# An adding transfer and one long scan in place of nine short ones, in a kernel of decayed attention and a mixture of experts

## The chip, the core and the metric

The kernel runs on one core of one Trainium2 chip. A core has five engines, each with its own queue of instructions: TensorE (PE, matrix products), VectorE (DVE), ScalarE (ACT, functions from loadable tables), GpSimd (POOL) and SyncE (SP, which only issues transfers). Sixteen DMA engines move data for all queues. Each engine works through its queue in order; between engines, semaphores order the work. The metric is the device time of one execution in microseconds (us), as the median of several runs.

## The reference

Thirty-two heads (4 batches of 8), 768 steps, 48 features. A complex decay per feature is kept below 0.999 in size; a state matrix per head decays and takes up k v^T at each step, and its real part is read with q:

```python
mag = np.sqrt(a_re * a_re + a_im * a_im)
scale = np.minimum(mag, 0.999) / (mag + 1e-06)
a_re_n, a_im_n = (a_re * scale, a_im * scale)
for t in range(S):
    ar, ai = (a_re_n[:, :, t, :, None], a_im_n[:, :, t, :, None])
    new_re = ar * S_re - ai * S_im
    new_im = ar * S_im + ai * S_re
    kv = np.einsum('bhd,bhe->bhde', k[:, :, t], v[:, :, t])
    S_re, S_im = (new_re + kv, new_im)
    y[:, :, t] = np.einsum('bhd,bhde->bhe', q[:, :, t], S_re)
```

The 3,072 rows of y (384 features) then go through eight experts with a capacity of 384 tokens each. Logits come from `x @ w_gate`; all (token, expert) pairs are walked in order of falling logit, and a pair is taken if the token is free and the expert has room. Each expert computes `relu(x @ w1) @ w2`.

## The kernel before

The attention works in chunks of 128 steps (a unit, 24 of them), three units to a group; two groups are a batch, eight groups (0 to 7) in all. For a group the four inputs a_re, a_im, k, q lie as [128 partitions, 3, 384 steps]: eight heads of 16 features on the partitions, three such blocks side by side.

Since the decay is a product over steps, the kernel works with logarithms: the sum of log sizes within a chunk and the sum of angles. The stages of a group have short names in `elementwise` (L341 on):

- F1, F2 (ACT): squares of ar into s1 and of ai into s2. F6: s2 += s1. F3, F4 (DVE): ar times ai into p, and the mark of a negative ar.
- F5, F7, F8 (ACT): logarithms and an exponential, from which F11 (DVE) makes the tangent of the angle in p.
- F9 (DVE): `zi` = -0.5 min(log(mag^2), 2 log 0.999), minus the log decay. F10 (ACT): s2 = exp(-0.5 log(mag^2)) x 1e-6, that is 1e-6 over the size, the small term that the 1e-6 of the reference's denominator brings. The log decay to be summed has these two terms, zi and s2.
- S (DVE, L386 to L392): for each unit of the group and each of the three blocks one scan of 128 columns, which adds zi and s2 to the running sum and begins at zero: nine scans for a whole group.
- G1, G2 (ACT): the exponentials of minus and plus that sum. G3, G5 (DVE): q and k times them. G4: the last column of each chunk, the decay of the whole chunk.
- A1 (ACT): arctangent; N0 (DVE): scans of the angle, 384 columns each; N1, N2 and T1 to T3: reduction of the angle, sine and cosine into CS.

Then, for each unit, RK and RQ (DVE, `f<-kq,CS`) turn k and q; K (SP, eight transfers `KQ<-f`, one a head) stacks them with 96 features on the partitions; SC, FL, ST, CA, MX, FN (PE) make the scores, transposes, state and output, with MK (`am<-sc,mask`) and WM (`W<-U,KQ`) on DVE and KC, XC, XE on ACT between them; LR takes the logits.

In six groups (1 to 6, `BY_DMA`) F6 is already no DVE instruction but a transfer from SBUF to SBUF that adds, issued on POOL (`s<-s` in the profile). Groups 0 and 7 are cut in two pieces (`CUTS`) and do F6 on DVE.

What sets the order: all stages are entered as operations with an engine, a cost, their predecessors and a priority (the chunk's number plus an offset from the table `OFF`, one entry for each kind of stage, L641). `in_order` (L173 on) plays them through: whenever an engine is free, the ready operation with the lowest priority goes next. The code is emitted in that order, and a `Queue` holds every engine to it. An adding transfer counts there as an operation of POOL of 7.5 us for a whole group. ACT's functions lie in two tables, one with logarithm and exponential and one with arctangent and sine; `PLAN` says which stages of which group share a loading. Where PE would be idle by the plan, matrix products on a constant (`hot`) are put in. The experts behind have a planner of their own, which the change leaves alone.

Of the kernel before, what the change touches and what calls it, by code (L numbers as in the profile page):

```python
# [8 lines left out]
F32 = mybir.dt.float32  # L9
# [4 lines left out]
AF = mybir.ActivationFunctionType  # L14
OP = mybir.AluOpType
# [5 lines left out]
B, H, S, D = 4, 8, 768, 48  # L21
# [3 lines left out]
GC = 3  # L25
# [210 lines left out]
def attention(nc, real, tc, z, q, k, a_re, a_im, v_tok, xd, later):  # L236
    ctx = ExitStack()
    con = ctx.enter_context(tc.tile_pool(name="acon", bufs=1))
# [4 lines left out]
    ps = ctx.enter_context(tc.tile_pool(name="ps", bufs=1, space=PSUM))  # L243
    W, VT = [], []
    v, g = nc.vector, nc.gpsimd
    for i in range(2):
        w = con.tile([96, 400], F32, name=f"W{i}")
        g.memset(w, 0.0)
        W.append(w)
    for i in range(2):  # L250
        x = con.tile([128, GC, 432], F32, name=f"V{i}")
# [9 lines left out]
    act = nc.scalar.activation  # L261
# [4 lines left out]
    def op(key, eng, cost, prio, fn, deps=()):  # L266
        kind = key[0][0] if type(key[0]) is tuple else key[0]
        o = Op(eng, cost, fn, [made.get(d) for d in deps], prio)
        o.kind = kind + ("<" if prio < EARLY else ">" if prio >= LATE else "")
        ops.append(o)  # L270
        made[key] = o
        return o
# [4 lines left out]
    def scan_(n):  # L277
        return n * 2.15 / 960 + 0.06
# [4 lines left out]
    def sca(n, bias=False):  # L283
        return n / 1200 + (0.23 if bias else 0.14)
# [4 lines left out]
    def dma(nbytes):  # L289
        return nbytes / 2.6e5  # L290
# [6 lines left out]
    def get(name, gi, shape=None, p=ew, **kw):  # L297
        if (name, gi) not in tiles:
            tiles[name, gi] = p.tile(shape or [128, 3, T], F32, name=name, **kw)
        return tiles[name, gi]  # L300

    BUFS = dict(ar=1, ai=1, kq=KQ_BUFS, s1=S1_BUFS, s2=2, zi=2, p=2, neg=2, gc=3, CS=1)

# [3 lines left out]
    def free(name, stages, gi):  # L307
        return [x for s in stages for x in last_of(s, gi - BUFS[name])]
# [4 lines left out]
    def load_a(gi, j, name, src):  # L313
        b, c0, n = GROUPS[gi]
        lo, hi = cuts[gi][j]
        w = slice(lo * 128, hi * 128)
        t = slice(c0 * 128 + lo * 128, c0 * 128 + hi * 128)
        return lambda: nc.sync.dma_start(
            get(name, gi, p=ld, bufs=1)[:, :, w], src[b, :, :, t].rearrange("j p t -> p j t"))
# [21 lines left out]
    def elementwise(gi, j, at):  # L341
        b, c0, _ = GROUPS[gi]
        lo, hi = cuts[gi][j]
        n = hi - lo
        N3 = 384 * n
# [3 lines left out]
        def G_(name, **kw):  # L349
            return get(name, gi, **kw)[..., cols]  # L350
# [4 lines left out]
        def add(stage, eng, cost, fn, deps):  # L355
            op((stage, gi, j), eng, cost, at, fn, deps)

        def k_(*ss):
            return [(s_, gi, j) for s_ in ss]

        add("li", "dma", dma(128 * N3 * 4), load_a(gi, j, "ai", a_im), free("ai", ["F2", "F3"], gi))
        add("la", "dma", dma(128 * N3 * 4), load_a(gi, j, "ar", a_re), free("ar", ["F1", "F3", "F4"], gi))
        add("F1", "act", sca(N3, True), lambda: act(G_("s1", bufs=S1_BUFS), G_("ar"), AF.Square, bias=z.cb[:, 0:1]),
            k_("la") + free("s1", ["F11", "F6"], gi))
# [7 lines left out]
            G_("neg", bufs=2), G_("ar"), 0.0, math.pi, op0=OP.is_lt, op1=OP.mult), k_("la") + free("neg", ["T1", "T2"], gi))  # L372
        if (gi, j) in BY_DMA:
            add("F6", "pool", 2.5 + 5.0 * n / GC, lambda: g.dma_start(out=G_("s2"), in_=G_("s1"), accum_op=OP.add), k_("F1", "F2"))
# [8 lines left out]
        add("F10", "act", sca(N3, True), lambda: act(G_("s2"), G_("s2"), AF.Exp, scale=-0.5, bias=z.cb[:, 3:4]), k_("F9"))  # L383
        add("F11", "dve", dve(N3), lambda: v.tensor_tensor(G_("p"), G_("p"), G_("s1"), op=OP.mult), k_("F8", "F3"))

        for c in range(n):  # L386
            def scan(c=c):
                t = slice(c * 128, c * 128 + 128)
                zi, s2 = G_("zi"), G_("s2")
                for i in range(3):  # L390
                    v.tensor_tensor_scan(zi[:, i, t], zi[:, i, t], s2[:, i, t], 0.0, op0=OP.add, op1=OP.add)
            add(("S", c), "dve", 3 * scan_(128), scan, k_("F10"))  # L392
        add("G1", "act", sca(N3), lambda: act(G_("s2"), G_("zi"), AF.Exp, scale=-1.0), [(("S", c), gi, j) for c in range(n)])
        add("G2", "act", sca(N3), lambda: act(G_("zi"), G_("zi"), AF.Exp), k_("G1"))
        add("G3", "dve", dve(N3), lambda: v.tensor_tensor(G_("kq")[:, 1], G_("kq")[:, 1], G_("s2"), op=OP.mult),
            k_("G1") + [("lk", gi)])
# [178 lines left out]
    for gi in range(G):  # L575
        for j in range(len(cuts[gi])):
            elementwise_at = gi * GC + cuts[gi][j][0]
            if j == 0:
                load(("lk", gi), 4.5, elementwise_at + 0.5, load_kq(gi), turned(gi - KQ_BUFS))
                if gi < 2:  # L580
                    load(("lv", gi), 2.2, elementwise_at + 0.6, load_v(gi))
            elementwise(gi, j, elementwise_at)
        for c in range(GC):
            turns(gi * GC + c)
            unit(gi * GC + c)
        if gi + 2 < G:
            load(("lv", gi + 2), 2.2, elementwise_at + 4, load_v(gi + 2),
                 [("MX", gi * GC + c) for c in range(GC)] + [("ST", gi * GC + c) for c in range(GC)])
# [8 lines left out]
    for o in ops:  # L597
        o.prio += OFF.get(o.kind, 0.0)
    hot = ps.tile([128, 512], F32, name="hot")
# [33 lines left out]
PLAN = [(0, 0, 1, 3), (0, 2, 1, 3), (2, 4, 3, 5), (4, 6, 5, 7), (6, 8, 7, 9), (8, 10, 9, 11), (10, 12, 11, 13), (12, 14, 13, 15), (14, 16, 15, 17), (16, 18, 17, 19)]  # L633
KQ_BUFS = 2
S1_BUFS = 2
BY_DMA = [(gi, 0) for gi in range(1, 7)]
SLACK = 0.0
DMA_WAIT = 1.5
DMA_DONE = 1.1
START = dict(pe=0.0, act=0.6, dve=1.5, pool=3.4, dma=0.0)  # L640
OFF = {"A1": 7.7532, "F1": -8.0, "F10": -0.2852, "F11": 6.1629, "F2": 1.0958, "F3": 3.1048, "F4": 3.0098, "F5": -8.0, "F6": 8.0, "F7": -6.5322, "F8": 3.2365, "F9": 5.0508, "FL": 2.946, "FL<": -3.9259, "FN": 4.3835, "G1": -0.6071, "G2": 4.4992, "G3": 8.0, "G4": -8.0, "G5": -5.9505, "K": 1.9006, "KC": -0.4768, "LR": -3.8173, "MK": -2.5243, "MX": -4.6482, "N0": 0.976, "N1": -8.0, "N2": -5.5169, "P0": -6.2872, "R0": -7.514, "R1": -4.516, "R2": 3.2639, "R3": 4.827, "R4": -4.8476, "R5": -0.5791, "S": 6.954, "SC": 3.4101, "SC<": -8.0, "ST": 0.3675, "ST<": -0.421, "T1": 7.9956, "T2": 6.9667, "T3": -8.0, "TL": 5.7027, "UA": -3.4084, "UA<": -5.1223, "WM": 0.1274, "XC": 7.799, "XC<": -7.3842, "XE": 4.4086, "XS": 0.7846, "la": -5.6357, "later": -8.0, "li": -5.3368, "lk": -1.3428, "lv": 6.2134, "RK": -2.7051, "RQ": -3.6666, "table": -0.5748, "CA": 3.7656, "BE": -7.9653}  # L641
CHAIN = ("scalar", "vector", "tensor", "gpsimd", "sync")
F_BUFS, KC_BUFS = 4, 5
SQ = ()
# [407 lines left out]
class Plan:  # L1052
# [13 lines left out]
    def add(self, eng, cost, outs, ins, fn):  # L1066
        deps = []
        for v, write in [(x, False) for x in ins] + [(x, True) for x in outs]:
            r = v.root
            for o, part, w in r.uses:  # L1070
                if (w or write) and (part is None or v.part is None or part == v.part):
                    deps.append(o)
            for old in r.older:
                deps += [u[0] for u in old.uses]
            if r.peer:
                deps.append(r.peer.uses[0][0])
        g = self.group
        if g is not None and g[0] is not None:
            o = g[0]
            assert o.eng == eng  # L1080
            o.deps += [d for d in deps if d is not o]
            o.cost += cost
            o.fns.append(fn)
        else:
            o = Op(eng, cost, None, deps, 0.0)
            o.fns = [fn]
            o.fn = lambda: [f() for f in o.fns]
            o.kind = self.kind
            self.ops.append(o)
            if g is not None:  # L1090
                g[0] = o
        for v, write in [(x, False) for x in ins] + [(x, True) for x in outs]:
            v.root.uses.append((o, v.part, write))
        return o
# [275 lines left out]
@with_exitstack  # L1370
def tile_decay_attention_then_capacity_moe(ctx, tc, q, k, a_re, a_im, v, w_gate, w1, w2, out):
    nc = tc.nc
    z = K()
    con = ctx.enter_context(tc.tile_pool(name="con", bufs=1))
    dp = ctx.enter_context(tc.tile_pool(name="dram", bufs=1, space=DRAM))
    xd = dp.tile([N, DM], F32)
    constants(nc, con, z, w_gate)
    router = Router(nc, z, con)
    queue = Queue(tc, nc, CHAIN)
    attention(queue, nc, tc, z, q, k, a_re, a_im, v, xd, router.constants())  # L1380
    experts(queue, tc, z, router, w1, w2, xd, out)
# [35 lines left out]
```

## Time and profile before

| | |
|---|---|
| median of 3 runs | 536.97 us (533.43 to 538.29) |
| the profiled execution | 535.22 us, span 533.4 us |
| busy, share of the span | PE 86%, DVE 79%, ACT 51%, POOL 16% |
| chain that ended last | PE 52%, DVE 16%, DMA 9%, issue 8%, ACT 5% |
| adding transfers `s<-s` | 6, of 576 KB each |
| first matrix product | 44.1 us |
| last logits of the attention | 244.2 us |

How to read what follows: the windows give, for stretches of the span, the busy time of each engine and the count of its instructions; the chain is followed back from the last instruction to what released it; a wait is put down to the one that came last. Instructions are named out<-in, with buffer numbers left out, so that `s` is s1 or s2. Nearly all carry L131, the line of the helper through which the queues pass; they are told apart by their names. Times of one instruction overlap the next by some 60 to 100 ns, so start-to-start is what a row of them costs.

### The profile page before, as it was taken

The numbers are of one execution on the slowest core, as the hardware profiler recorded it, in microseconds if no ns is written. First come the engines' busy times: TensorE is split into PE (matmuls) and PEld (weight loads), VectorE is DVE, ScalarE is ACT, GpSimd is POOL, SyncE is SP. The second block draws the span as 40 slices with busy tenths as digits, with TensorE's granted clock in tenths as the row PEclk, the third lists the DMA queues.
The fourth block names the chain that finished last, engine by engine and source line by source line (L and its number), as shares of the span: only waits on it lengthen the run. The fifth ranks groups of instructions, "written<-read, shape, count | busy, mean of one in ns | idle before, by whom it ended". The sixth has DMA issues, their size and how long they took to land.

```text
span 533.4 us, 9780 instructions
## 1 busy us (share of the span) xinstructions
PE 456.6 (86%) x3665; PEld 402.6 (75%) x3665; DVE 424.0 (79%) x1249; ACT 274.2 (51%) x426; POOL 84.5 (16%) x96
## 2 busy tenths in 40 slices
PE   0008989998989999995599898999999999999993
PEld 0007978686869889994498567898888888999993
DVE  8988689999989999835847779899898998944340
ACT  6995678796949695521012512342261723633430
POOL 3000000000000000000021322232341414620202
PEclk9999999999989999997589999999999999999998
DMA  7866858887978676621353403552260714830101
GB/s 226 264 182 156 222 164 270 224 228 245 257 216 267 197 237 169 192 75 45 110 174 123 173 31 122 190 215 82 78 250 29 265 34 190 320 138 4 45 1 44
DMA packets 48911, 86.06 MB, mean 161 GB/s; under 512 B 5344, under 2 KB 43744, under 8 KB 46816
## 3 DMA queue, kind: packets, MB, share of 16 engines
q1 hardware_dynamic: 39104, 42.56, 27.4%
q0 software_dynamic: 6304, 38.16, 21.2%
q10 hardware_dynamic: 3456, 4.72, 2.6%
q8 instruction: 29, 0.48, 0.4%
q14 instruction: 18, 0.15, 0.1%
HBM read 53.49 MB, written 9.44 MB: 118 GB/s over the span
## 4 chain that ended last, share of the span: by engine, by line
PE 52%; DVE 16%; DMA 9%; issue 8%; ACT 5%; SPq 4%; POOL 3%; POOLq 0%; DVEq 0%; ACTq 0%
PE acc L131 29%; PE y L131 5%; PE U L131 5%; PE sc L131 5%; SPq L131 4%; DMA s<-s 3%; DMA KQ<-f 3%; PE cnt L131 3%; ACT s L131 2%; DVE f L131 2%; PE xp L131 2%; PE kp L131 2%; DMA ai<-in_a_im 2%; DVE hl L131 1%; PE thr L131 1%
## 5 line engine op out<-in xcount | busy, mean ns | idle before, releaser
L131 PE MATMUL sc<-KQ 96*128 96x128 f32 x384 | 52.8, 293 | 41.7 <-DMA KQ<-f 41.6
L131 PEld LDWEIGHTS sc<-KQ 96*128 96x128 f32 x384 | 50.0, 207 | 45.1 <-DMA KQ<-f 42.6
L131 ACT ACTIVATE hh<-acc 128x384 fp32r<-128x384 f32 x56 | 27.4, 491 | 63.3 <-PE acc L131 61.9
L131 PE MATMUL acc<-w2l,hh 128*128 128x384 f32 x168 | 54.1, 346 | 0.0
L131 PE MATMUL acc<-w2h,hh 128*128 128x384 f32 x168 | 53.6, 345 | 0.0
L131 PE MATMUL acc<-w2h,hl 128*128 128x384 f32 x168 | 53.4, 343 | 0.0
L131 PE MATMUL acc<-xl,w1h 128*128 128x384 f32 x168 | 51.4, 344 | 0.0
L131 PE MATMUL acc<-xh,w1h 128*128 128x384 f32 x168 | 51.3, 345 | 0.0
L131 PE MATMUL acc<-xh,w1l 128*128 128x384 f32 x168 | 51.1, 343 | 0.0
L131 POOL DMA_INDIRECT out<-ot,idx x24 | 31.5, 1310 | 112.2 <-ACT ot L131 102.6
L131 DVE SCALAR_TENSOR_TENSOR hl<-acc,hh 128x384 fp32r<-128x384 f32 x56 | 30.4, 551 | 17.8 <-ACT hh L131 17.2
L131 DVE TENSOR_TENSOR f<-kq,CS 128x768 f32<-128x768 f32 x48 | 43.5, 951 | 0.2 <-ACT CS L131 0.2
L131 ACT ACTIVATE ot<-acc 128x384 f32<-128x384 f32 x24 | 11.7, 489 | 58.4 <-PE acc L131 50.1
L131 PE MATMUL y<-am,V 128*64 128x128 f32 x384 | 38.3, 289 | 1.1 <-ACT xT L131 0.6
L131 DVE TENSOR_TENSOR am<-sc,mask 128x512 f32<-128x512 f32 x48 | 32.2, 684 | 8.9 <-PE sc L131 8.8
L131 DVE TENSOR_TENSOR ind<-m,thr 128x768 bf16<-128x768 f32 (+1 forms) x40 | 33.7, 848 | 6.0 <-PE thr L131 5.8
L131 POOL DMA_INDIRECT w1t<-in_w,eidx x8 | 9.3, 1164 | 162.0 <-DVE of L131 118.7
L131 PE MATMUL U<-V,kt 128*96 128x48 f32 x320 | 32.4, 258 | 1.6 <-DVE tl L131 1.3
L131 PEld LDWEIGHTS U<-V,kt 128*96 128x96 f32 x320 | 31.6, 176 | 2.6 <-ACT kt L131 1.8
L131 PEld LDWEIGHTS acc<-xh,w1h 128*128 128x128 f32 x168 | 30.8, 188 | 2.6 <-issue 1.1
L131 PE MATMUL y<-KQ,W 96*64 96x128 f32 x320 | 31.8, 276 | 0.2 <-DVE W L131 0.2
L131 PEld LDWEIGHTS acc<-w2h,hh 128*128 128x128 f32 x168 | 31.1, 188 | 0.7 <-issue 0.4
(197 smaller groups left out, 1108.1 us busy)
## 6 DMA issues: line engine op xcount, KB each, us to landing
KQ<-f SPq DMA_DIRECT2D x192, 96.4 KB, 2.5
kq<-in_k SPq DMA_DIRECT2D x8, 576.0 KB, 5.1
kq<-in_q SPq DMA_DIRECT2D x8, 576.0 KB, 7.0
V<-in_v SPq DMA_DIRECT2D x8, 576.0 KB, 8.9
xd<-x ACTq DMA_DIRECT2D x24, 192.0 KB, 2.8
ar<-in_a_re SPq DMA_DIRECT2D x6, 576.0 KB, 4.6
ai<-in_a_im SPq DMA_DIRECT2D x6, 576.0 KB, 5.4
s<-s POOLq DMA_DIRECT2D x6, 576.0 KB
```

What stands on the lines that cost most here:

```text
L131: r = f(*a, **k)
```

## The change

In groups 1 to 6 (`SUM_BY_DMA`) the two terms of the log decay are summed ahead of the scan, by a second adding transfer on POOL: SD, zi += s2, behind F10. One scan over all 1,152 columns then takes the place of the nine. It multiplies the running sum by a constant, `again`, and adds zi; `again` is one everywhere and zero in the first column of each chunk, so that the sum begins anew there. G1 waits for this scan. The constant is filled on POOL at the start of the attention. The table of offsets is new throughout, with an entry for SD, so the order within the attention changes on all engines.

```diff
+    again = con.tile([128, 9 * 128], F32, name="again")
+    g.memset(again, 1.0)
+    g.memset(again.rearrange("p (a t) -> p a t", t=128)[:, :, 0], 0.0)
...
-        for c in range(n):
+        summed = (gi, j) in SUM_BY_DMA
+        if summed:
+            add("SD", "pool", 2.5 + 5.0 * n / GC, lambda: g.dma_start(out=G_("zi"), in_=G_("s2"), accum_op=OP.add), k_("F10"))
+
+            def scan_all():
+                x = G_("zi").rearrange("p a t -> p (a t)")
+                v.tensor_tensor_scan(x, again, x, 0.0, op0=OP.mult, op1=OP.add)
+            add(("S", 0), "dve", scan_(N3) + 0.12, scan_all, k_("SD"))
+        for c in range(0 if summed else n):
...
-        add("G1", "act", sca(N3), lambda: act(G_("s2"), G_("zi"), AF.Exp, scale=-1.0), [(("S", c), gi, j) for c in range(n)])
+        add("G1", "act", sca(N3), lambda: act(G_("s2"), G_("zi"), AF.Exp, scale=-1.0), [(("S", c), gi, j) for c in range(1 if summed else n)])
...
+SUM_BY_DMA = [(gi, 0) for gi in range(1, 7)]
...
-OFF = {"A1": 7.7532, "F1": -8.0, "F10": -0.2852, "F11": 6.1629, "F2": 1.0958, "F3": 3.1048, "F4": 3.0098,
...
+OFF = {"A1": 8.0, "F1": -1.706, "F10": -7.9433, "F11": 6.3823, "F2": -0.1719, "F3": 3.6663, "F4": 2.2339,
...
```

More of the change, by code (lines that the diff above doesn't have):

```diff
@@ L640 @@
 START = dict(pe=0.0, act=0.6, dve=1.5, pool=3.4, dma=0.0)
-OFF = {"A1": 7.7532, "F1": -8.0, "F10": -0.2852, "F11": 6.1629, "F2": 1.0958, "F3": 3.1048, "F4": 3.0098, "F5": -8.0, "F6": 8.0, "F7": -6.5322, "F8": 3.2365, "F9": 5.0508, "FL": 2.946, "FL<": -3.9259, "FN": 4.3835, "G1": -0.6071, "G2": 4.4992, "G3": 8.0, "G4": -8.0, "G5": -5.9505, "K": 1.9006, "KC": -0.4768, "LR": -3.8173, "MK": -2.5243, "MX": -4.6482, "N0": 0.976, "N1": -8.0, "N2": -5.5169, "P0": -6.2872, "R0": -7.514, "R1": -4.516, "R2": 3.2639, "R3": 4.827, "R4": -4.8476, "R5": -0.5791, "S": 6.954, "SC": 3.4101, "SC<": -8.0, "ST": 0.3675, "ST<": -0.421, "T1": 7.9956, "T2": 6.9667, "T3": -8.0, "TL": 5.7027, "UA": -3.4084, "UA<": -5.1223, "WM": 0.1274, "XC": 7.799, "XC<": -7.3842, "XE": 4.4086, "XS": 0.7846, "la": -5.6357, "later": -8.0, "li": -5.3368, "lk": -1.3428, "lv": 6.2134, "RK": -2.7051, "RQ": -3.6666, "table": -0.5748, "CA": 3.7656, "BE": -7.9653}
+OFF = {"A1": 8.0, "F1": -1.706, "F10": -7.9433, "F11": 6.3823, "F2": -0.1719, "F3": 3.6663, "F4": 2.2339, "F5": -7.7649, "F6": 5.849, "F7": 6.5769, "F8": -3.2078, "F9": 2.6695, "FL": 1.2547, "FL<": 8.0, "FN": 4.2725, "G1": -3.6349, "G2": -1.218, "G3": 7.3854, "G4": -3.8733, "G5": -4.3477, "K": 2.785, "KC": 1.3113, "LR": 0.9742, "MK": -0.6582, "MX": -7.3883, "N0": 1.9427, "N1": -6.0423, "N2": -8.0, "P0": 2.6412, "R0": -0.5866, "R1": -0.9225, "R2": -6.3991, "R3": 0.0469, "R4": -4.5019, "R5": 8.0, "S": 6.3482, "SC": 2.5769, "SC<": 6.1603, "ST": -3.0459, "ST<": -4.9702, "T1": 6.4264, "T2": -0.4648, "T3": -4.7434, "TL": 5.7714, "UA": -7.8876, "UA<": -0.6213, "WM": 0.079, "XC": 8.0, "XC<": 0.7027, "XE": 2.1979, "XS": 4.141, "la": -5.959, "later": 2.3562, "li": -5.1343, "lk": 1.3753, "lv": 4.4034, "RK": -2.0242, "RQ": -3.022, "table": -7.0509, "CA": 1.9062, "BE": -5.3127, "SD": 8.0}
 CHAIN = ("scalar", "vector", "tensor", "gpsimd", "sync")
```

## The prediction

> **What bounds the kernel now.** I read the windows by stage first, then the chain of waits, then who VectorE (DVE) waits for, then single instructions. The change sits in the attention part, which ends near 245 us of the 533.4 us span; the expert part behind it keeps its instructions, so only the first 245 us can move. Windows of 20 us (engine, busy us, instruction count; then granted clock, share of the 16 DMA engines, GB/s):
>
> ```profile
> core 0: us, PE busy (x) PEld busy (x) DVE busy (x) ACT busy (x) POOL busy (x), PEclk, DMA share, GB/s
> 40.00:60.00 20.00, 18.27 (x100) 16.74 (x102) 16.17 (x28) 14.08 (x16) 0.00 (x0) 1.00 0.71 198
> 60.00:80.00 20.00, 18.18 (x175) 15.70 (x173) 15.72 (x28) 12.14 (x17) 0.84 (x1) 1.00 0.65 163
> 80.00:100.00 20.00, 19.27 (x199) 15.77 (x199) 19.69 (x34) 18.00 (x20) 0.85 (x1) 1.00 0.92 275
> ...
> 140.00:160.00 20.00, 17.31 (x155) 14.42 (x154) 18.12 (x33) 13.08 (x16) 0.85 (x1) 0.91 0.83 231
> ...
> 220.00:240.00 20.00, 20.00 (x232) 18.30 (x228) 9.14 (x17) 5.62 (x12) 0.00 (x0) 1.00 0.41 110
> ```
>
> Three stages. From 40 to 80 us no engine is full: DVE idles 3.8 and 4.3 us. From 80 to about 200 DVE is nearly full. From 220 DVE is done and TensorE (PE) is full. The chain of waits shows the same (start, duration, what):
>
> ```profile
> 18.34 8.09 DMA s<-s
> ...
> 44.12 2.50 PE sc L131 x10
> ...
> 141.12 9.25 DMA s<-s
> ...
> 215.39 1.78 PE sc L131 x16
> ...
> 222.82 1.81 PE sc L131 x16
> 230.26 1.78 PE sc L131 x16
> ```
>
> Up to 44.1 the chain is latency, one adding transfer of 8.09 us in it. At the end the units of 128 tokens follow each other every 7.43 us (215.39, 222.82, 230.26), set by PE alone: the 24 units would fill 24 x 7.43 = 178 us, and attention takes some 200 us from 44.1. So about 20 us are DVE work and waits, and only these can shrink.
>
> **The change part by part.**
>
> *Nine scans become one.* DVE groups between 44 and 222 us, and a small scan from the whole span:
>
> ```profile
> L131 DVE TENSOR_TENSOR_SCAN zi<-zi,s 128x128 f32<-128x128 f32 x54 | 18.1, 400 | 0.0
> L131 DVE TENSOR_TENSOR_SCAN neg<-p,neg 128x384 f32<-128x384 f32 x9 | 7.9, 935 | 0.0
> ...
> L131 DVE TENSOR_TENSOR_SCAN rank<-ones,of,tie 128x24 f32<-128x24 f32 x7 | 1.8, 260 | 0.0
> ```
>
> The 54 scans cost 18.1 us, 0.335 each and 3.02 per group. One of 384 columns costs 7.9/9 = 0.878, so a column costs (0.878 - 0.335)/256 = 2.12 ns, and 1,152 columns 0.878 + 768 x 0.00212 = 2.51 us. Saved: 0.51 a group, 3.1 us in six. If the long scan only did as well as three of 384 (2.63), it would be 2.3. The new scan multiplies and adds; the `rank` scan is of that kind, and its 260 ns lie above the 400 - 104 x 2.12 = 180 that 24 columns of the other kind would take, so a start may cost 0.08 more, once a group. All columns are walked either way, so only starts are saved. Four of the six stand in the full stretch (2.0 of the 3.1), the first two among DVE's waits; I take **-3.1**, with the 2.0 as a bound.
>
> *The mask of ones.* It is filled on GpSimd (POOL) ahead of all its other constants:
>
> ```order
>  L59 ISA
>  L59 IOTA jp 128x128
>  L81 DMA pick<-in_w_gate 48x4x8 x2
> -L131 MEMSET W_110 96x400
> -L131 MEMSET W_112 96x400
> -L131 MEMSET V_114 128x3x48
> -L131 MEMSET V_116 128x3x48
> +L131 MEMSET again 128x1152
> +L131 MEMSET again 128x9
> +L131 MEMSET W_113 96x400
> +L131 MEMSET W_115 96x400
> +L131 MEMSET V_117 128x3x48
> ```
>
> So everything behind moves back by two fills, the ramp `jf` among it, for which DVE waits already:
>
> ```profile
> 3.15 0.85 POOL L131 MEMSET W<- 96x400 f32 x2
> 3.89 0.43 POOL L131 MEMSET V<- 128x144 f32 x2
> ...
> 5.22 0.15 POOL L131 IOTA jf<- 2x32 f32 x1
> ...
> 5.41 0.19 DVE L131 TENSOR_SCALAR start<-jf 1x32 bf16<-1x32 f32 x1 [0.20 <-POOL jf L131]
> ```
>
> ```profile
> 28.66 0.51 ACT L131 ACTIVATE p<-neg 128x384 f32<-128x384 int32 x1
> ```
>
> Two fills of 400 columns take 3.89 - 3.15 = 0.74, so 1,152 columns about 0.37 x 2.88 = 1.07, 1.1 with the second. Queued behind DVE's `start` is all of DVE's work on the first pieces, which leads through ScalarE (ACT) to the adding transfer of 18.34. Bounds for the first KQ: 0 (ACT absorbs it) to +1.1. One activation of 0.51 that stood behind that transfer's landing now stands ahead of it, so **+0.7**.
>
> *The transfer, and the scan's wait for it.* SD needs F10, and the scan needs SD. What an adding transfer costs by itself shows where the DMA engines carry nothing else (30 to 36 us, 40 slices, tenths; then the queue's share):
>
> ```profile
> 30.52 0.85 POOL L131 DMA_DIRECT2D s<-s  x1 [11.12 <-ACT s L131]
> ```
>
> ```profile
> DMA  0000000000001919699093990919969010000000
> ...
> q0 software_dynamic: 144, 0.59, 51.0%
> ```
>
> It takes 51% of 6 us, 3.06 us of all 16 engines, and is over in slice 33, at 35.0: landing 4.5 us after POOL began. Among other traffic the two of the chain took 8.09 and 9.25. DVE runs in order, so the question is how much work stands between F9 (`zi<-s`, after which ACT does F10) and the scan. The tightest place is group 5. Its DVE rows before, from F9 to the first scan (s_970 is its s2, now s_1040):
>
> ```order
> L131 TENSOR_SCALAR zi<-s_970 128x1152
> L131 COPY f<-gc 128x6
> L131 TENSOR_TENSOR p<-p,s_1034 128x1152
> L131 TENSOR_TENSOR W_110<-U,KQ 96x384
> L131 SCALAR_TENSOR_TENSOR zi<-zi,s_970 128x128 x3
> ```
>
> The same stretch of DVE now, from F9 to the scan:
>
> ```order
> L131 TENSOR_SCALAR zi<-s_1040 128x1152
> L131 COPY tl<-neg 128x3
> L131 TENSOR_TENSOR kq<-kq,s_758 128x1152
> L131 TENSOR_SCALAR neg<-neg 128x1152
> L131 COPY f<-gc 128x6
> L131 TENSOR_SCALAR neg<-neg 128x1152
> L131 TENSOR_TENSOR p<-p,s_984 128x1152
> L131 TENSOR_TENSOR W_113<-U,KQ 96x384
> L131 TENSOR_TENSOR am<-sc,mask 128x512 x2
> L131 TENSOR_TENSOR W_115<-U,KQ 96x384
> L131 SCALAR_TENSOR_TENSOR p<-ar,ai 128x1152
> L131 SCALAR_TENSOR_TENSOR zi<-again,zi 128x1152
> ```
>
> Three rows stood between the two, now ten. What these take, start to start, with F10 on ACT:
>
> ```profile
> 81.91 0.55 DVE L131 TENSOR_TENSOR W<-U,KQ 96x384 f32<-96x384 f32 x1
> 82.38 1.35 DVE L131 TENSOR_TENSOR kq<-kq,s 128x1152 f32<-128x1152 f32 x1
> 83.64 0.75 DVE L131 TENSOR_SCALAR zi<-s 128x1152 f32<-128x1152 f32 x1
> 84.31 1.35 DVE L131 TENSOR_TENSOR p<-p,s 128x1152 f32<-128x1152 f32 x1
> 85.58 1.28 DVE L131 TENSOR_TENSOR am<-sc,mask 128x512 f32<-128x512 f32 x2
> 86.78 1.05 DVE L131 TENSOR_TENSOR_SCAN zi<-zi,s 128x128 f32<-128x128 f32 x3
> ```
>
> ```profile
> 84.43 1.26 ACT L131 ACTIVATE s<-s,cb 128x1152 f32<-128x1152 f32 x1
> ```
>
> W 0.47, kq 1.26, a tensor_scalar 0.67, p 1.27, two am 1.20: between F9 and the scan of group 5 stand kq, two neg, two p, two W, two am and two copies (about 0.07 each), 1.26 + 1.34 + 2.54 + 0.94 + 1.20 + 0.14 = 7.4 us. F10 and landing need 1.3 + 4.5 = 5.8 at best, 1.3 + 8.1 = 9.4 or 1.3 + 9.25 = 10.6 among traffic. So DVE waits 0, 2.0 or 3.2 us, with the rotations f of the next units and their KQ transfers queued behind. For group 4 the same count gives 9.6 us of cover (wait 0 to 1.0), for group 2 10.2 (0 to 0.4); groups 1, 3 and 6 have far more. (For group 4: four am, one scan, W, p, two kq, four copies, one lg; group 2 has one neg more.) Together 0 to +4.6. The stretch is as loaded as that of the chain's two; I take the lower of them, **+2.0**. The Trainium skill, page "DMA: Bandwidth & Descriptors", section on the anatomy of a GpSimd DMA, gives 2.0 us plus bytes/436e9 for one: an estimate of 3.4 us for 589,824 bytes, by which no scan waits and the sum would be 2.0 lower. The 8.09 and 9.25 of this trace speak against it where the engines are loaded. On POOL each SD stands ahead of a later group's F6, but its F10 comes before that group's F2 on ACT, so F6 waits for nothing new.
>
> *The new order.* All priorities are new. DVE rows where group 1's rotations begin, before:
>
> ```order
> L131 TENSOR_TENSOR f<-kq,CS 128x6x128
> L131 TENSOR_TENSOR am<-sc,mask 128x512 x2
> L131 TENSOR_REDUCE lg<-xp 128x8
> L131 TENSOR_TENSOR f<-kq,CS 128x6x128 x2
> L131 TENSOR_TENSOR W_110<-U,KQ 96x384
> ```
>
> The same place now:
>
> ```order
> L131 TENSOR_TENSOR f<-kq,CS 128x6x128 x3
> L131 TENSOR_TENSOR am<-sc,mask 128x512 x2
> L131 TENSOR_REDUCE lg<-xp 128x8
> L131 TENSOR_TENSOR f<-kq,CS 128x6x128 x2
> L131 TENSOR_TENSOR W_115<-U,KQ 96x384
> ```
>
> A unit's KQ needs two f. All three f at the head now run together. Before, the second came after a wait for PE (instructions by start, duration):
>
> ```profile
> 62.06 0.95 DVE L131 TENSOR_TENSOR f<-kq,CS 128x768 f32<-128x768 f32 x1
> ...
> 67.10 1.82 DVE L131 TENSOR_TENSOR f<-kq,CS 128x768 f32<-128x768 f32 x2
> ...
> 68.07 8.27 SPq L131 DMA_DIRECT2D KQ<-f  x12
> ```
>
> Who DVE waited for between 44 and 80 us (total, times, longest):
>
> ```profile
> DVE am L131 <- PE sc L131: 4.7, 4, 2.2
> DVE W L131 <- PE U L131: 1.6, 1, 1.6
> DVE lg L131 <- ACT x L131: 1.5, 2, 1.4
> ```
>
> Now it ends at 62.06 + 2 x 0.87 = 63.8 instead of 68.0, so PE gets unit 3 up to 4.2 us earlier, out of the 7.8 us that DVE waits in 44 to 80 (the last three rows). Gain 0 to 4.2: ACT's tables and the loads must keep up too, so half, **-2.1**. Unit 0 loses a little, since the scan of group 1 now stands between its two am; that is inside the half. On SP one load now goes ahead of unit 2's KQ, one issue.
>
> *More traffic.* Six transfers of 3.06 us add 18.4 us of all 16 engines.
>
> ```profile
> 80.00:180.00 100.00, 94.12 (x923) 78.98 (x923) 94.69 (x166) 82.15 (x100) 2.54 (x3) 0.98 0.84 241
> ```
>
> Four fall here: share 0.84 + 0.12 = 0.96. Cost 0 if the pipeline's five KQ buffers cover it; upper bound in the rivals. I take **+0.5**.
>
> **Sum:** -3.1 + 0.7 + 2.0 - 2.1 + 0.5 = -2.0. The profiled execution took 535.22 us (span 533.4), 1.75 below the median of 536.97. Against its own time the sum gives 533.2; against the median, which the forecast is for, **535.0**.
>
> **The rivals.**
>
> *The adds land early (faster).* With 4.5 us no scan waits, and the lead of 4.2 us is kept whole: -3.1 + 0.7 - 4.2 = -6.6, **530.4**. For it: the transfer alone is that quick, and cover is 7.4 us or more. Against it: the share of 0.84 to 0.92 where it must land. The page's 3.4 us stands for this rival.
>
> *The DMA engines become the bound (slower).* Between 141 and 151 us the share was full, and the KQ transfers showed it (first row; the second is the whole span):
>
> ```profile
> KQ<-f SPq DMA_DIRECT2D x6, 96.4 KB, 6.4
> ...
> KQ<-f SPq DMA_DIRECT2D x192, 96.4 KB, 2.5
> ```
>
> They landed in 6.4 us instead of 2.5, and PE lost 20 - 17.31 = 2.7 us in the window around it, at a clock of 0.91. If each of the four adds between 80 and 180 makes such a place, it costs 4 x 2.7 = 10.8: 10.8 + 0.7 - 3.1 = +8.4, **545.4**; with two of them, 540. It decides once the share passes 1.0 for longer than five KQ buffers last. The Trainium skill, same page, section "Issuing engines are not separate DMA queues", says that transfers issued from different engines interleave on the same 16; the 6.4 agrees.
>
> *Nothing moves.* DVE's freed time is handed to waits for PE, 94.12 of 100 us busy above: **537**.
>
> **Chances.** Forecast 0.45 (its own range 531.5 to 538.5), early landing 0.22, DMA bound 0.20, nothing 0.13. About 1%, 5.4 us, is what a measurement can tell from no change. Faster than 531.6: 0.20 of the early landing and 0.05 of the forecast's edge, 0.25. Slower than 542.3: 0.16 of the DMA rival and 0.02 of the edge, 0.18. Within: 0.57. The range 529 to 543 leaves out about 0.1 on each side.
>
> **What would show it.** Right: one scan near 2.5 us; a DVE wait of about 2 us for the transfer at group 5's scan and little at the others; DVE's `start` about 1.1 us later; the burst of KQ for unit 3 some 2 to 4 us earlier against the first PE work; PE's 7.43 us at the end unchanged. Wrong: a scan above 3 us; waits at all six scans or KQ landing in over 4 us, which would make the time the DMA rival's; or first PE work moved by more than 2 us, since the first 44 us were followed only by the first KQ.

## The result

The changed kernel took 549.59 us (median of 4, 546.29 to 550.41) beside 537.63 us for the kernel before (533.43 to 540.08): a ratio of 1.0255, 95% interval 1.0203 to 1.0306. It is slower by some 13 us, where 535.0 was forecast and 543 was the upper end of the range. Its profiled execution took 549.47 us (span 547.6).

All of it lies in the attention part. The last reduction of the logits, in the timeline of VectorE, kernel before first and changed kernel second:

```profile
244.46 0.31 DVE L131 TENSOR_REDUCE ext<-lg 128x1 f32<-128x48 f32 x2
```

```profile
258.55 0.31 DVE L131 TENSOR_REDUCE ext<-lg 128x1 f32<-128x48 f32 x2
```

It comes 14.1 us later; the spans differ by 14.2. The rotations f, which feed the K and Q transfers, start 1.1 us later and end 14 us later (kernel before, then changed kernel; first and last start at the end of the row's numbers):

```profile
L131 DVE TENSOR_TENSOR f<-kq,CS x48: 926/952/960, 36.2 to 225.8; 128x768 f32<-128x768 f32 x48
```

```profile
L131 DVE TENSOR_TENSOR f<-kq,CS x48: 933/950/960, 37.3 to 240.0; 128x768 f32<-128x768 f32 x48
```

The parts that the change names look as forecast. Groups of instructions of the changed kernel (busy us and mean ns, then idle time ahead of them), then VectorE's waits in the first 260 us (total, times, longest), changed kernel and kernel before:

```profile
L131 DVE TENSOR_TENSOR_SCAN zi<-again,zi 128x1152 f32<-128x1152 f32 x6 | 15.3, 2551 | 2.8 <-DMA zi<-s 2.8
```

```profile
DVE lg L131 <- ACT x L131: 13.0, 10, 3.4
DVE am L131 <- PE sc L131: 10.5, 15, 3.1
...
DVE zi L131 <- DMA zi<-s: 2.8, 2, 1.7
...
DVE open L131 <- POOL wd L131: 1.8, 1, 1.8
```

```profile
DVE am L131 <- PE sc L131: 8.8, 12, 2.2
DVE lg L131 <- ACT x L131: 8.3, 8, 2.8
```

The long scan takes 2.55 us, and two of the six wait for their transfer, 2.8 us in all. The two largest waits are for ScalarE and TensorE, and these grew, from 8.3 and 8.8 to 13.0 and 10.5 us. So the loss is spread. The windows of the changed kernel show where (busy us of PE, PEld, DVE, ACT, POOL with counts; granted clock, share of the DMA engines, GB/s):

```profile
40.00:60.00 20.00, 16.79 (x142) 14.51 (x142) 19.78 (x25) 14.66 (x17) 0.85 (x1) 1.00 0.85 210
60.00:80.00 20.00, 17.93 (x150) 15.46 (x149) 16.79 (x27) 13.38 (x18) 0.85 (x1) 0.85 0.90 250
80.00:100.00 20.00, 19.36 (x183) 16.60 (x182) 15.49 (x23) 15.06 (x18) 2.15 (x2) 0.89 0.83 225
...
140.00:160.00 20.00, 12.88 (x123) 9.96 (x125) 15.27 (x19) 13.19 (x15) 0.86 (x1) 0.98 0.97 264
...
220.00:240.00 20.00, 20.00 (x219) 18.68 (x217) 17.66 (x39) 16.08 (x27) 0.00 (x0) 1.00 0.57 158
```

```profile
80.00:180.00 100.00, 85.74 (x809) 71.25 (x813) 81.34 (x119) 72.93 (x87) 6.43 (x7) 0.94 0.86 233
```

In 80 to 180 us VectorE did 81.3 us of work instead of 94.7, TensorE 85.7 instead of 94.1. The DMA engines' share is 0.86, where it was 0.84 before and 0.96 had been expected. Four transfers were added here and the mean share hardly rose, since less of the other work was done in the same time. The chain of waits of the changed kernel shows one such place (start, duration, what):

```profile
136.16 9.63 DMA zi<-s
145.82 2.56 DVE zi L131
148.38 0.85 DVE f L131
149.32 0.88 DVE f L131
152.08 7.46 DMA KQ<-f
159.99 1.25 ACT s L131
161.78 2.04 PE xp L131 x8
...
181.11 6.79 DMA KQ<-f
```

Group 5's adding transfer is under way for 9.6 us, then the scan and two rotations follow, then K and Q are under way for 7.5 us, and ScalarE stands until these have landed, with a store of x next in its queue and the copy that TensorE needs behind that. TensorE stood still for 6.8 us. The waits of both in this stretch, and the median landing of the two kinds of transfer over the whole kernel:

```profile
ACT s L131 <- DMA KQ<-f: 6.3, 1, 6.3
```

```profile
PE xp L131 <- ACT xT L131: 6.8, 1, 6.8
PE xp L131 <- DVE lg L131: 2.7, 1, 2.7
```

```profile
KQ<-f SPq DMA_DIRECT2D x192, 96.4 KB, 2.7
...
zi<-s POOLq DMA_DIRECT2D x6, 576.0 KB, 7.9
```

### The profile page after: what moved, and what is told of

It is laid out like the page before. It is cut to its first block, busy times and chain, and to the rows that moved or that the text cites. A ratio compares the mean times of both kernels' runs of the same rounds, so it can differ in the third digit from the quotient of the medians.

```text
span 547.6 us, 9736 instructions
## 1 busy us (share of the span) xinstructions
PE 457.2 (83%) x3652; PEld 401.1 (73%) x3664; DVE 421.2 (77%) x1201; ACT 275.0 (50%) x426; POOL 90.9 (17%) x104
## 4 chain that ended last, share of the span: by engine, by line
PE 46%; issue 21%; DVE 15%; DMA 6%; ACT 4%; POOL 4%; SPq 2%; POOLq 0%; ACTq 0%; DVEq 0%
PE acc L131 29%; PE sc L131 3%; PE y L131 3%; PE U L131 3%; DMA KQ<-f 3%; PE cnt L131 2%; SPq L131 2%; PE xp L131 2%; DMA zi<-s 2%; DVE f L131 2%; ACT s L131 2%; DMA ar<-in_a_re 2%; DVE hl L131 1%; PE thr L131 1%; DVE zi L131 1%
## 5 line engine op out<-in xcount | busy, mean ns | idle before, releaser
L131 PE MATMUL sc<-KQ 96*128 96x128 f32 x384 | 52.2, 290 | 44.2 <-DMA KQ<-f 44.1
L131 PEld LDWEIGHTS sc<-KQ 96*128 96x128 f32 x384 | 48.8, 202 | 47.3 <-DMA KQ<-f 45.3
L131 PE MATMUL xp<-pick,xT 112*128 112x104 f32 x192 | 28.2, 293 | 14.8 <-ACT xT L131 10.2
L131 DVE TENSOR_TENSOR am<-sc,mask 128x512 f32<-128x512 f32 x48 | 32.2, 684 | 10.6 <-PE sc L131 10.5
L131 PEld LDWEIGHTS xp<-pick,xT 112*128 112x128 f32 x192 | 24.9, 202 | 19.8 <-ACT xT L131 13.2
L131 ACT ACTIVATE s<-s,cb 128x1152 f32<-128x1152 f32 (+2 forms) x20 | 21.1, 1057 | 25.5 <-DVE zi L131 12.6
```

The costliest lines, as they stand in the source:

```text
L131: r = f(*a, **k)
```

## The experiments

Ratios are to the kernel before, timed beside each kernel on the same chip; with 95% intervals. The kernel before itself took 534.6 to 540.0 us there (its medians on four chips), so ratios and not microseconds are compared between kernels.

### Is it the new order?

First guess: the new table of priorities makes an order in which ScalarE stands at its own stores (theory A), or else the transfers themselves cost it (theory B). Four kernels were run.

The mechanism with the table of before:

```diff
-OFF = {"A1": 8.0, "F1": -1.706, ...
+OFF = {"A1": 7.7532, "F1": -8.0, ...
```

> The transfer and the long scan stay, the table of offsets is that of before (SD has none, so 0). Theory A (the new table's order costs, by ACT standing at its own stores of x until KQ transfers have landed): the profile shows ACT waiting at most 6 us for KQ and xd transfers between 40 and 262 us (before 5.6, after 17), and the time is 535 to 541. Theory B (the six added transfers cost, by their wait and their load): 545 to 552, as after, with KQ landing above 2.6 us in the median and scan waits of 2 us or more in sum.

The new table with the operations of before:

```diff
-SUM_BY_DMA = [(gi, 0) for gi in range(1, 7)]
+SUM_BY_DMA = []
```

> The new table, but no group sums by transfer: nine scans, no SD, no mask wait. Theory A: still 543 to 552, with ACT held at its stores for 10 us or more. Theory B: 534 to 540. The planner places work anew here, so that a value between 540 and 543 tells neither.

The changed order on every engine, with the six transfers left out:

```diff
-lambda: g.dma_start(out=G_("zi"), in_=G_("s2"), accum_op=OP.add)
+lambda: None
```

> The order of the changed kernel, instruction for instruction, with the six SD transfers left out: the scan sums zi alone, so the small term s2 of the log decay is missing from the output in groups 1 to 6, and the scan waits for F9 only. Theory A: 545 or more, since the order of ACT and SP is unchanged; the gain is the 2.8 us of scan waits at most. Theory B: 534 to 541, with KQ landing back at 2.5 us and ACT held at its stores no longer than in the kernel before (6 us).

The changed kernel with its 24 stores moved to another queue:

```diff
-            nc.scalar.dma_start(xd[i * 128:i * 128 + 128], ...
+            nc.gpsimd.dma_start(xd[i * 128:i * 128 + 128], ...
```

> The changed kernel with the 24 stores of x issued from POOL instead of ACT, all else in the same order. Theory A: ACT's waits for KQ and xd transfers (17 us in the changed kernel) go, and the time falls by 7 to 13, to 537 to 543. Theory B: within 3 us of the changed kernel (546 to 552), as another wait takes their place.

Measured: old table 570.48 us (559.73 to 573.62, beside 534.62; too scattered for a ratio), new table with nine scans 563.38 us (ratio 1.0538, 1.0491 to 1.0585), no transfer 543.29 us (1.0163, 1.0118 to 1.0209), stores on GpSimd 549.08 us (1.0249, 1.0197 to 1.0301). The first two fit neither theory: a table put to other operations makes a third, worse order, and says nothing about the order that it was made for. So an order has to be kept as it is, and the instructions changed in place. The fourth speaks against A: ScalarE no longer waits for K and Q, and nothing is gained. The third left 6 us with the transfers and 9 with the rest; the next runs take the rest apart.

### Order, scan, fill and load, one at a time

In place means: same order on every engine, only the named instructions differ.

Before's order, one long scan where the last of the nine stood, no transfer, the mask filled behind the constant `cold`:

```diff
+                if (gi, j) in SUM_BY_DMA:
+                    if c == n - 1:
+                        x = zi.rearrange("p a t -> p (a t)")
+                        v.tensor_tensor_scan(x, again, x, 0.0, op0=OP.mult, op1=OP.add)
+                    return
                 for i in range(3):
                     v.tensor_tensor_scan(zi[:, i, t], zi[:, i, t], s2[:, i, t], 0.0, op0=OP.add, op1=OP.add)
```

> The order of the kernel before, op for op, with one scan of 1,152 columns where the last of its nine stood in groups 1 to 6; no transfer, and the mask is filled behind the other constants of GpSimd. Left out: in groups 1 to 6 the second term of the decay isn't added. Theory O (the new order itself loses time, whatever it is made of): the old order keeps its time or gains the scans' 3 us, 531 to 535 us, some 10 us below the same work in the new order (543.3 us without transfers). Theory S (the one scan upsets the loop between VectorE and ScalarE, because nothing downstream can start until all of it is done, while the nine let work between them): about as slow as the new order without transfers, 541 to 545 us.

The changed order with nine scans in place of the one, no transfer, no mask:

```diff
-                v.tensor_tensor_scan(x, again, x, 0.0, op0=OP.mult, op1=OP.add)
+                for c in range(n):
+                    t = slice(c * 128, c * 128 + 128)
+                    for i in range(3):
+                        v.tensor_tensor_scan(zi[:, i, t], zi[:, i, t], s2[:, i, t], 0.0, op0=OP.add, op1=OP.add)
```

> The changed kernel's order, op for op, with the nine scans of 128 emitted where its one scan stands, and no adding transfer; everything is computed. Theory O (the new order itself loses time): 543.3 us (the new order without transfers) and up to 3 us for the longer scans, 543 to 547 us. Theory S (the one scan is at fault): back near the kernel before, 534 to 538 us.

The changed order with transfers of the same size that nothing waits for (their target `spare` is filled behind `cold`):

```diff
+            def beside():
+                g.tensor_copy(spare[:, 0:1], G_("s2")[:, 0, 0:1])
+                g.dma_start(out=spare, in_=again, accum_op=OP.add)
-            add("SD", ..., lambda: g.dma_start(out=G_("zi"), in_=G_("s2"), accum_op=OP.add), k_("F10"))
+            add("SD", ..., beside, k_("F10"))
```

> The changed kernel's order, with the six adding transfers of 576 KB issued at their places, once F10's result is there, but from the constant mask into a spare tile, so that no scan waits for them: the traffic without the wait. Left out: in groups 1 to 6 the second term of the decay isn't added. Theory W (the 6.3 us that the transfers cost are the scans' waits, 2.8 us in the trace, and what follows from them): 543 to 545 us. Theory L (they are the load: the KQ transfers and the first adding transfer land later): 547 to 550 us.

The changed kernel with its mask filled behind `cold`:

```diff
     g.memset(cold, 0.0)
+    g.memset(again, 1.0)
+    g.memset(again.rearrange("p (a t) -> p a t", t=128)[:, :, 0], 0.0)
```

> The changed kernel with the mask filled behind all of GpSimd's other constants. Theory (the 1.1 us that the start shows is lost for good): 548.5 us, 1.1 below the changed kernel's 549.6. Rival (work at the start has slack that the later waits take up): 549.6 us, no change.

And the two cross-checks of scan and fill, both without transfers (one scan, with the fill behind group 1's first adding transfer; nine scans, with the fill at the start):

```diff
+            def both():
+                g.dma_start(out=G_("s2"), in_=G_("s1"), accum_op=OP.add)
+                if gi == 1:
+                    g.memset(again, 1.0)
...
```

> The changed kernel's order with its one scan and without its six added transfers, with the mask filled while GpSimd stands idle behind group 1's first adding transfer (about 20 us) and not at the start. Left out: in groups 1 to 6 the second term of the decay isn't added. With the nine scans in place of the one, and no mask, the same order took 537.5 us; with the mask filled at the start and the one scan, 543.3 us. Theory F (the fill at the start makes the 6 us): 536 to 538 us. Theory S (the one scan makes them): 541 to 544 us.

> The changed kernel's order with nine scans of 128 in place of each long one and no added transfers, and the mask filled at the start as in the changed kernel, though nothing reads it; everything is computed. Theory F (the fill at the start makes the 6 us): 541 to 544 us. Theory S: 537.5 us and the 1.1 us of the fill, 538 to 539.5 us.

And before's kernel with the traffic beside it:

```diff
+                if (gi, j) in BY_DMA and c == 0:
+                    g.tensor_copy(spare[:, 0:1], s2[:, 0, 0:1])
+                    g.dma_start(out=spare, in_=again, accum_op=OP.add)
                 for i in range(3):
                     v.tensor_tensor_scan(zi[:, i, t], zi[:, i, t], s2[:, i, t], 0.0, op0=OP.add, op1=OP.add)
```

> The kernel before, with its order and its nine scans, and beside it six adding transfers of 576 KB from one spare tile to another, issued by GpSimd once F10's result of groups 1 to 6 is there; nothing waits for them, and everything is computed. Theory L (the load of the transfers costs in any order): 542 to 547 us, 7 to 10 us over the kernel before, as in the new order (552.8 against 543.3 us). Rival (the new order alone is hurt, since its K and Q transfers stand closer): 536 to 539 us.

| kernel | order | scan | added transfers | ratio, interval |
|---|---|---|---|---|
| old order, one scan | before | one, mask ahead of the ramp | none | 1.0078, 1.0029 to 1.0127 |
| new order, nine scans | changed | nine | none | 1.0036, 0.9994 to 1.0077 |
| nine scans and fill | changed | nine, mask at the start | none | 1.0024, 0.9968 to 1.0080 |
| no transfer, no early fill | changed | one, mask at 20 us | none | 1.0017, 0.9963 to 1.0072 |
| no transfer (above) | changed | one, mask at the start | none | 1.0163, 1.0118 to 1.0209 |
| traffic beside | changed | one | 6, nothing waits | 1.0302, 1.0232 to 1.0373 |
| changed kernel, late fill | changed | one | 6 | 1.0269, 1.0177 to 1.0360 |
| old order, traffic | before | nine | 6, nothing waits | 1.0241, 1.0149 to 1.0332 |
| changed kernel | changed | one | 6 | 1.0255, 1.0203 to 1.0306 |

The new order by itself is neutral (1.0036). The transfers by themselves, in the untouched order of before and with no one waiting for them, cost what the change costs: 1.0241 against 1.0255. With the wait taken away in the new order, nothing came back (1.0302; the fill of `spare` moves this kernel's start back by another 1.0 us), so the 2.8 us of waiting scans don't explain it.

The late fill tested less than it was meant to: the ramp `jf` that VectorE waits for still stood behind the fill, at 6.4 us as in the changed kernel (5.2 in the kernel before). The same holds for the old order with one scan, so its 0.8% is one scan and fill together.

One row doesn't fit: one scan with the mask filled at the start gave 1.0163, and with the fill moved to 20 us 1.0017, though the fill alone (1.0024) and the one scan alone (1.0017) cost nothing there. The traces show where the first of these two loses. Between the logits of units 5 and 6 it falls back by 5.7 us (96.17 to 115.57 us, beside 93.90 to 107.60), and in that stretch its granted clock is 0.50 (early mask first, then the mask at 20 us):

```profile
104.00:108.00 4.00, 4.00 (x29) 3.67 (x29) 2.31 (x3) 1.79 (x4) 0.00 (x0) 0.50 1.06 349
```

```profile
104.00:108.00 4.00, 3.94 (x45) 3.17 (x46) 3.26 (x8) 3.97 (x5) 0.00 (x0) 1.00 0.90 280
```

The ten executions with the mask at 20 us span 533.5 to 544.9 us, with mean granted clocks from 0.966 down to 0.942; the four with the early mask (541.5 to 545.1, 0.942 to 0.949) lie at the slow end of that span. So the row may be a matter of the clock and not of scan and fill, but the two kernels were timed on different chips, and this is not shown. Until it is, the transfers' part in the changed kernel lies between 0.9% (over 1.0163) and 2.4% (over 1.0017), some 5 to 13 us.

How the load acts can be read from the DMA view of two neighbouring stretches of 10 us. Before's order with the traffic, at 94 and at 104 us (40 slices, share in tenths; then the K and Q transfers issued there, and their median landing):

```profile
DMA  9989899899997999999899999999989999999969
...
KQ<-f SPq DMA_DIRECT2D x7, 96.4 KB, 6.1
...
ai<-in_a_im SPq DMA_DIRECT2D x1, 576.0 KB, 11.0
```

```profile
DMA  8495100799849457100000383773845838548398
...
KQ<-f SPq DMA_DIRECT2D x11, 96.4 KB, 2.3
```

The kernel before, the first of the two stretches:

```profile
DMA  9999997998999797999999977476010393683745
...
KQ<-f SPq DMA_DIRECT2D x13, 96.4 KB, 3.4
```

The engines were already full for the first 6 us. The added transfer stretches that to all 10 us, in which 7 instead of 13 K and Q transfers were issued, at 6.1 instead of 3.4 us to land. ScalarE, with a store of x next in its queue, stood until the load `ai` had landed, and TensorE stood for the copy that ScalarE had behind it (waits of the kernel with the traffic, 94 to 110 us):

```profile
PE xp L131 <- ACT xT L131: 6.0, 1, 6.0
ACT xT L131 <- DMA ai<-in_a_im: 5.1, 1, 5.1
```

Behind that little is ready to be sent, and the engines stand half empty. So, in this pair of stretches, the mean share hides it: the load comes in bursts that set the pace, and what is added lengthens the burst. The transfers were issued by GpSimd and touched no tile of the computation, and yet SyncE's landed later. The Trainium skill (page "DMA: Bandwidth & Descriptors", section "Issuing engines are not separate DMA queues") says that transfers issued by different engines run on the same 16 DMA engines and interleave. The trace agrees, with 6.1 against 3.4 us.

### Is it the clock behind each stall?

In the changed kernel the granted clock falls to one half behind TensorE's long stalls. Windows of 4 us:

```profile
72.00:76.00 4.00, 3.49 (x20) 3.16 (x21) 1.64 (x4) 1.25 (x3) 0.00 (x0) 0.75 0.65 165
76.00:80.00 4.00, 4.00 (x29) 3.91 (x29) 3.15 (x7) 0.98 (x1) 0.00 (x0) 0.50 0.84 243
80.00:84.00 4.00, 4.00 (x35) 3.67 (x32) 1.78 (x4) 0.46 (x2) 1.30 (x1) 0.50 0.52 120
...
160.00:164.00 4.00, 2.04 (x8) 1.96 (x10) 0.99 (x2) 1.87 (x3) 0.00 (x0) 0.50 0.83 250
```

If that is what makes a short wait dear (theory C), idle matmuls in the stalls should bring the time back:

```diff
+KEEP = {("FN", 2): 3, ("FL", 3, 0): 4, ("FN", 11): 24, ("FN", 14): 9}
...
+            for _ in range(getattr(o, "warm", 0)):
+                nc.tensor.matmul(hot, cold[:, :128], cold, start=True, stop=True)
```

> The changed kernel with 40 more idle matmuls of 128 x 512 on TensorE, none of which anything reads, ahead of the four places at which TensorE stood longest: 3 ahead of unit 2's and 24 ahead of unit 11's multiplication by pick, 9 ahead of unit 14's, and 4 ahead of unit 3's first transposes. Theory C (a stall of TensorE costs more than its own length, since the granted clock falls to 0.5 behind it and TensorE then runs at half speed: 74 to 84 us, 160 to 166 us and 190 to 193 us in the trace, 20 us at half clock against 3 in the kernel before): the clock stays at 1.0 there, and up to half of 17 us comes back, 541 to 546 us. Rival (the other engines set the end, and TensorE catches up anyway): 548 to 551 us, whatever the clock does.

The same windows of this kernel:

```profile
72.00:76.00 4.00, 3.73 (x32) 3.16 (x31) 3.35 (x7) 1.30 (x4) 0.00 (x0) 1.00 0.64 160
76.00:80.00 4.00, 4.00 (x57) 3.77 (x56) 4.00 (x9) 1.60 (x3) 0.59 (x1) 1.00 0.84 248
...
148.00:152.00 4.00, 3.43 (x15) 3.50 (x17) 3.58 (x6) 1.83 (x2) 0.00 (x0) 0.50 1.03 332
...
160.00:164.00 4.00, 4.00 (x25) 2.36 (x23) 0.39 (x1) 0.66 (x3) 0.00 (x0) 1.00 0.67 199
```

In the stretches of 72 to 84 and 160 to 164 us the clock stayed at 1.00, and the time was 552.64 us (1.0278, 1.0188 to 1.0368): nothing gained. But at unit 14 it still fell (0.57 at 192 to 196 us), and it fell at new places, as at 148 us, where the changed kernel has 1.00; the mean over 80 to 180 us is 0.95 instead of 0.94. So theory C finds no support here, but the run did not keep the clock up as a whole, and how much the half clock adds to each stall stays open.

### What of the transfers costs, and does less load give it back?

All in the order of before. Half the size, a plain copy, and next to nothing:

```diff
-g.dma_start(out=spare, in_=again, accum_op=OP.add)
+g.dma_start(out=spare[:, :576], in_=again[:, :576], accum_op=OP.add)
+g.dma_start(out=spare, in_=again)
+g.dma_start(out=spare[:, :2], in_=again[:, :2], accum_op=OP.add)
```

> The kernel before with six adding transfers beside it of half the size, 288 KB each, that nothing waits for; everything is computed. At full size they cost a ratio of 1.024, some 13 us. Theory B (the cost goes with what they move): 1.012, 6 to 7 us over the kernel before. Rival T (each transfer costs as such, by its issue on GpSimd or its start): 1.02 and more, 11 to 13 us. Rival K (there is a knee, and half the load is still hidden): 1.00 to 1.005, 0 to 3 us.

> The kernel before with six plain copies of 576 KB beside it, from the same tile to the same tile, from the same queue, and without adding; everything is computed. Theory B (bytes written are what counts): as with adding, a ratio of 1.02 to 1.03. Rival A (adding is what is dear, since each packet is read and written at its target): under 1.012, less than half of the 13 us.

> The kernel before with the same six added transfers beside it, at the same places and with the same fills and the same small copy on GpSimd ahead of each, but of 2 columns (1 KB) each; everything is computed. Theory E (the cost is the time that the transfers take of the 16 DMA engines: 18.4 us in six at full size, 9.2 at half size or without adding, and 1.024, 1.018 and 1.015 in time): next to none of it is left, a ratio of 1.00 to 1.005. Rival T (each transfer costs as such; the line through full and half size leaves 1.012 at no size): 1.009 to 1.015.

Between 30 and 40 us the queue of GpSimd carries one of the kernel's own adding transfers and one added one. Its share of those 10 us, for the full size, half size, plain copy and 1 KB in this order:

```profile
q0 software_dynamic: 288, 1.18, 64.4%
```

```profile
q0 software_dynamic: 288, 0.88, 47.7%
```

```profile
q0 software_dynamic: 288, 1.18, 45.9%
```

```profile
q0 software_dynamic: 288, 0.59, 33.5%
```

Less the last one, an added transfer takes 3.1, 1.4 and 1.2 us of all 16 engines. Adding is dear: at the same size it takes two and a half times the engine time of copying. The ratios rise with the engine time: 1.0241 (18.5 us in six), 1.0184, 1.0089 to 1.0279 (8.5 us), 1.0154, 1.0072 to 1.0236 (7.4 us). They don't rise in proportion, and neither half size nor plain copy met the value expected of a cost by bytes (1.012; 1.02 to 1.03); the intervals overlap, so that bytes and engine time aren't told apart by the kernel's time. The transfers of 1 KB took 541.29 us (533.53 to 543.51) beside 537.26 (531.81 to 548.82), 1.0075 by the medians and with no interval, since both scattered. By these medians some 9 of the 13 us go with what the transfers move, and up to 4 may be a price for issuing six transfers as such; whether that is so, this run can't tell.

Last, the kernel before with its own six adding transfers (`s<-s`) turned into additions, on GpSimd and on VectorE, at the same places:

```diff
-lambda: g.dma_start(out=G_("s2"), in_=G_("s1"), accum_op=OP.add)
+lambda: v.tensor_tensor(G_("s2"), G_("s2"), G_("s1"), op=OP.add)
```

> The kernel before, in its order, with the six adding transfers that it has already (the two terms ahead of the logarithm, groups 1 to 6) replaced by six additions on GpSimd at the same places of its queue; everything is computed. Theory L (the attention part is bound by the DMA engines, so that a load taken away gives as much as one added costs): 522 to 530 us, 6 to 13 us under the kernel before. Rival (the kernel before lies below the knee, and its transfers are hidden): 533 to 540 us, no gain. Rival (GpSimd's addition takes longer than the transfer or holds VectorE up): 540 to 550 us.

> The kernel before, in its order, with its six adding transfers replaced by six additions of 1,152 columns on VectorE, at some 1.3 us each; everything is computed. Theory L (load taken away gives as much as load added costs, 13 us, less up to 8 us of VectorE): 525 to 534 us. Rival (the load of the kernel before is hidden, and VectorE is full from 80 to 200 us): 538 to 546 us.

> The additions on VectorE once more, with more rounds: 0.9959 before, with an interval from 0.9915 to 1.0004. If the gain is real, 0.990 to 0.998; if not, 0.998 to 1.004. The first run's traces had the last logits of attention at 239.7 us against 244.5.

GpSimd's addition takes 2.87 us and gave 1.0011 (0.9964 to 1.0058), where 522 to 530 us was expected if load taken away gave as much as load added costs; it took 538.86. That gain did not come, but the run isn't clean: beside five of the six additions, VectorE's work took some 2 us longer. Two of these places (in the kernel before, such a row of three scans took 1.05 us and such a tensor_scalar 0.75):

```profile
18.71 3.43 DVE L131 TENSOR_TENSOR_SCAN zi<-zi,s 128x128 f32<-128x128 f32 x3
...
30.10 2.90 DVE L131 TENSOR_SCALAR zi<-s 128x1152 f32<-128x1152 f32 x1
```

VectorE's addition gave 0.9959 (0.9915 to 1.0004), and with more executions 531.67 us, 0.9900 (0.9863 to 0.9936). The profiled execution of that last run was disturbed (1,519.69 us) and isn't read; its other six took 530.27 to 535.21 us. The earlier run's middle stretch and end of attention (its fastest execution, 529.51 us):

```profile
80.00:180.00 100.00, 93.69 (x937) 79.28 (x940) 98.83 (x173) 81.39 (x99) 0.00 (x0) 1.00 0.78 225
```

```profile
239.74 0.31 DVE L131 TENSOR_REDUCE ext<-lg 128x1 f32<-128x48 f32 x2
```

VectorE is fuller (98.8 of 100 us against 94.7), the share of the DMA engines is 0.78 instead of 0.84, and the attention ends 4.7 us earlier. The opposite of the change, more work on the fullest engine and less on the transfers, is the version that beats both kernels, if only by 0.4 and 1.0% in its two runs.

## Why the prediction was wrong

- **Nine scans become one (-3.1).** Per scan right: 2.55 us measured, 2.51 forecast; 2.8 us less work in six. In the kernel's time it can't be found: with no transfers, one scan and nine stand at 1.0017 and 1.0036 in the changed order.
- **The mask (+0.7).** The trace has the first rotation 1.1 us later. TensorE's first score product starts at 43.07 instead of 40.64 us, and its first sixteen end 1.2 us later (the 44.1 us of the table of before is where the chain takes them up, not the first of them). In the kernel's time the fill alone is below what can be measured (1.0024 with it, 1.0036 without). The 1.0163 of fill and one scan together remains open.
- **The waits (+2.0).** 2.8 us in two waits, 1.7 at group 5 and 1.2 at group 4, where 2.0 and 0 to 1.0 were forecast. But this was not where the time went: without them the kernel was no faster (1.0302).
- **The new order (-2.1).** The three f at the head of group 1 run together as forecast, and end at 64.6 us instead of 68.9:

```profile
61.87 2.69 DVE L131 TENSOR_TENSOR f<-kq,CS 128x768 f32<-128x768 f32 x3
```

  The order alone gave 1.0036: the lead was worth nothing measurable.
- **More traffic (+0.5): this step failed.** It said that the share would rise to 0.96 and that five K and Q buffers would cover it, at a cost of 0.5 us. In the order of before, the same transfers with nothing waiting for them cost 13 us (1.0241); in the changed order it is 5 to 13, by which row one starts from. The working took a mean share of 0.84 over 100 us as 16 us of room. In the stretch shown above the room lies behind the burst, when little is ready to be sent. The rows were at hand: K and Q landing in 6.4 us with a full share, quoted under the rivals.
- **The rivals.** "The DMA engines become the bound" had the right mechanism and 0.20 of the chance; its price of four places at 2.7 us gave 545.4, 4 us too little. "The adds land early" fails at its condition: they landed in 7.9 us in the median, where it took 4.5 us, and two scans waited. The estimate of 3.4 us, from the Trainium skill's page "DMA: Bandwidth & Descriptors", section on the anatomy of a GpSimd DMA, is further off among this traffic.

Of the signs named beforehand, those of the single steps mostly came true, the scan's duration, the wait at group 5 and the earlier burst among them; the one for the DMA rival, landing in over 4 us, showed only locally (7.46 and 6.79 us in the chain), while the median over all K and Q rose from 2.5 to 2.7. A sign of being wrong, TensorE's first work moved by more than 2 us, came true by its start (2.4). A median over 192 transfers was too coarse a sign for a loss at a few places.

## What to carry to other kernels

A mean share of the DMA engines below 1 need not be room: look at slices of a quarter of a microsecond, and if the engines are full in bursts that the compute waits for, price an added transfer at its engine time (here 18.5 us for six, of which 5 to 13 came through), not at zero. Here moving work from a full engine to transfers took far more engine time than the 2.8 us that it freed. To tell a changed order from a changed operation, keep the order and change the instructions in place; a priority table put to other operations makes an order of its own.

## What the runs showed of the hardware

- An adding transfer between tiles of 576 KB takes 3.1 us of all 16 engines, a plain copy of the same size 1.2 us.
- After TensorE has stood for 2 to 7 us in the changed kernel, the granted clock is 0.50 for 3 to 10 us; in the changed order without transfers it is 0.50 for 20 us (99 to 119), with TensorE counted busy all the while. Idle matmuls ahead of three of four long stalls held it at 1.00 there, and no time was gained.
- GpSimd adds two tiles of 1,152 float32 columns in 2.87 us. VectorE's instructions beside it took some 2 us longer (3.43 instead of 1.05 us, 2.90 instead of 0.75); in place of an adding transfer the kernel's time was the same (1.0011).
